# Moving one group's loads, transpositions and cluster steps half a unit and more later in a fused attention and FFN kernel

## Chip, cores, metric

The kernel runs on one core of a Trainium2 chip. The metric is the time of one execution on the device in microseconds (us). The kernel before has a median of 328.62 us over 13 runs (327.7 to 329.52).

## What is computed

Routing attention over 4 batches of 8 heads, 768 positions, head size 64, and then a gated FFN over the 3072 tokens (512 to 1536 to 512):

```python
q_assign = np.argmax(np.einsum('bhsd,hcd->bhsc', q_n, c_n), axis=-1)
k_assign = np.argmax(np.einsum('bhsd,hcd->bhsc', k_n, c_n), axis=-1)
mask = q_assign[:, :, :, None] == k_assign[:, :, None, :]
scores = scale * np.matmul(q, k.transpose(0, 1, 3, 2))
scores = np.where(mask, scores, -1000000000.0)
attn = softmax(scores)
x = np.matmul(attn, v)            # heads side by side: (3072, 512)
xn = x / rms(x) * rms_g
g = xn @ w_gate
out = (g * sigmoid(g) * (xn @ w_val)) @ w_out
```

A query sees only keys of its own cluster, one of 16 for each head. The kernel gets the mask by appending a one-hot row of the cluster to q and to k, so that one matmul of 64 + 16 rows gives score and mask together.

## The kernel before, in words

All counting is from 0. There are 32 heads, n = 0 to 31, in 8 **groups** g of four, so that batch b has groups 2b and 2b+1. There are 8 **units** u: unit u is half of the queries (384) of batch u // 2, with all eight heads. Unit u therefore needs the groups of batch u // 2, both of them. The "fifth group" is g = 4, heads 16 to 19, first needed by unit 4. The "second unit" is u = 1.

The program writes out the order of every engine by hand. One call of `attention` (L659) runs through the 24 **gaps** of a unit: at each gap TensorE gets a pair of score matmuls (L348, three pairs a head), ScalarE the exp of them (L352), and in between comes the probability times v of the head before (`pv`, L366, 18 matmuls). Two heads share one accumulator `acc` in PSUM, of which there is one. VectorE empties it when both heads are in: reciprocal `inv` (L371) and product `x` (L373). The `pv` of the next pair cannot start before that.

Between the score pairs a list called `fill` is laid out. Each entry is a weight and a function, and entries are taken as long as their summed weight keeps step with the gaps. In unit u it holds, in this order:

1. the last eight gate/val items of the FFN of unit u-2 (f = 8 to 11): `gv`, L444, followed on VectorE by L453 (`th`) and L457 (`gvT`), with ScalarE's tanh (L452) between
2. `rms(u-1)`: ScalarE's squares (L393), VectorE's small steps (L400, L144 to L153) and the three products `xn` (L403), and then on SP's queue the x transposition, a DMA from `xn` to `xnT` (L406)
3. loads of heads listed in `LATE`
4. the output projection of unit u-2, nine items (`out_mm`, L469), whose result ScalarE copies (L472) and SP stores (L473)
5. the first sixteen gate/val items of unit u-1.

The preparation of group g = u + 2 is spread among these. It has **rows** and **clusters**. The sixteen rows are, for each head, two transpositions on VectorE (`trans`, L217, for heads from 14 on; they wait for the head's loads), then casts on POOL into the bf16 operands `qext` and `kext` (L240) and of v (L243), and with them SP's loads of v for head n + 4 and of q and k for head n + 6 (`load_v`, L107; `load_qk`, L96, eight DMAs a head of 48 KB each). Six staging buffers hold q and k. The clusters are, for q and for k: the products with the centroids on TensorE (`sc`, L254), a transposition (L257), the maximum (L262), a comparison (L266), a scaling for k (L285) and a transposition back (`oh`, L286) on VectorE, and sixteen small DMAs on POOL's queue that put the one-hot rows into `qext` and `kext` (`place`, L297).

The gate, val, o, and sc results share three PSUM buffers (`gen`), which are used in turn. Group 3 is prepared in unit 1, with its last steps at the head of unit 2. The three parts of `wo`, the last weight, are loaded on POOL's queue (L207) in unit 1 too.

The lines that the change touches decide where the parts of a group's preparation go:

```python
LATE = [19] + [n for n in range(20, B * H) if n % HG < 2]        # L58
if u == 2:                                                       # L703
    fill = fill[:1] + spread(fill[1:], [(0.0, f) for _, f in a3[5:]])
n = 12 if u == 2 else len(rows)                                  # L708
fill += spread(o, rows[:n]) + spread(ffn[:CUT], [(0.0, f) for _, f in rows[n:]] + clusters)
```

`spread(a, b)` lays the entries of b evenly among those of a. So in unit 2 twelve of the rows stand in the output projection and four with the clusters in the FFN part, and in later units all sixteen stand in the output projection.

Of the kernel before, what the change touches and what calls it, by code (L numbers as in the profile page):

```python
# [22 lines left out]
def kernel(  # L23
# [13 lines left out]
    B, H, S, D = q.shape  # L37
# [7 lines left out]
    HG = 4  # L45
# [8 lines left out]
    CUT = 2 * FC - 8  # L54
    LEAD = 6
    NQ, NV = 6, 8
    AV = 4
    LATE = [19] + [n for n in range(20, B * H) if n % HG < 2]  # L58
    BH = 14
    BG = BH // HG  # L60

# [22 lines left out]
    def load(n, part, on=None):  # L84
        if n not in staged:
            staged[n] = stage.tile([P, 2, ST, D], F32, tag="qk", name="qk")
        if n < BH:
            (on or nc.sync).dma_start(out=staged[n][:, part], in_=src((q, k)[part], n))
            return

        to = staged[n][:, part].rearrange("p t d -> p (t d)").rearrange("p (i r d) -> p i r d", i=HT, d=32)
        of = (q, k)[part][n // H, n % H].rearrange("(r p i e) (c d) -> e c p i r d", p=32, i=HT, e=2, d=32)
        for e in range(2):
            for c in range(2):
                r = 32 * (2 * e + c)
                nc.sync.dma_start(out=to[r:r + 32], in_=of[e, c])  # L96

    def load_qk(n):
        if n < B * H:
            load(n, 0)  # L100
            load(n, 1)

    def load_v(n, vq=None):
        if n >= B * H:
            return
        stagedv[n] = stage.tile([P, ST, D], F32, tag="vs", name="vs", bufs=NV)
        (vq or nc.sync).dma_start(out=stagedv[n], in_=src(v, n))  # L107
# [98 lines left out]
    def load_o(c):  # L206
        nc.gpsimd.dma_start(out=wo[:, c:c + 4], in_=moe_w_out[c * P:(c + 4) * P].rearrange("(c p) f -> p c f", p=P))  # L207
# [4 lines left out]
    def trans(g, h, part, on=None):  # L212
        if (g, h // 2) not in qkT:
            qkT[g, h // 2] = qk32.tile([P, 2, 2, UQ], F32, tag="qkT", name="qkT")
        qk = staged[g * HG + h]
        if g * HG + h >= BH:
            nc.vector.transpose(qkT[g, h // 2][:, h % 2, part], qk[:, part].rearrange("p t d -> p (t d)"))  # L217
            return
        ps = ps_g.tile([P, UQ], F32, tag="gen", name="tq")
        for i in range(HT):  # L220
            nc.tensor.transpose(ps[:, i * P:(i + 1) * P], qk[:, part, 2 * i:2 * i + 2].rearrange("p t d -> p (t d)"),
                                ident_f)
        to, by = qkT[g, h // 2][:, h % 2, part], 1.0 / ZS if part and g < BG else 1.0
        if on is nc.vector:
            nc.vector.tensor_scalar_mul(to, ps, by)  # L225
        else:
            nc.scalar.activation(to, ps, ACT.Copy, scale=by)
# [5 lines left out]
    def cast(on, g, h, part, es=(0, 1)):  # L233
        for e in es:
            to = cols((kext if part else qext)[g % 4][:D, h], g, e)
            of = qkT[g, h // 2][e * D:(e + 1) * D, h % 2, part]
            if on is nc.scalar:
                nc.scalar.copy(to, of)
            else:
                on.tensor_copy(to, of)  # L240

    def vcast(n):
        nc.gpsimd.tensor_copy(vbf[n // HG % 4][:, n % HG, :, :D], stagedv[n])  # L243
# [24 lines left out]
    def cluster_steps(g, m):  # L268

        of = {}  # L270

        def products():
            of["cl"] = cluster_products(g, [(h, m) for h in range(HG)])

        def most():
            of["mx"] = largest(of["cl"])

        def same():
            of["ohT"] = asg.tile([P, UQ], BF16, tag="ohT", name="ohT", bufs=2)
            compare(of["ohT"].rearrange("p (b e c) -> p b e c", e=2, c=NC), of["cl"], of["mx"])  # L280

        def back():
            put[g, m] = asg.tile([P, UQ], BF16, tag="oh", name="oh", bufs=3)
            if m and g >= BG:
                nc.vector.tensor_scalar_mul(of["ohT"], of["ohT"], ZS)  # L285
            nc.vector.transpose(put[g, m], of["ohT"])  # L286

        return [products, most, same, back]
# [3 lines left out]
    def place(on, g, m, es=(0, 1)):  # L292

        ext = (kext if m else qext)[g % 4]
        for h in range(HG):
            for e in es:
                on.dma_start(out=ext[D:D + NC, h, e * UQ:(e + 1) * UQ],  # L297
                             in_=put[g, m][32 * h + e * NC:32 * h + (e + 1) * NC])
# [190 lines left out]
    def group_work(g):  # L489

        t, c = [], []
        for h in range(HG):
            n = g * HG + h
            w = 0.0 if n >= BH else 0.3
            t += [(w, lambda h=h: trans(g, h, 0)), (w, lambda h=h: trans(g, h, 1))]

            def others(n=n):
                vcast(n)
                load_v(n + AV)
                if n + NQ not in LATE:  # L500
                    load_qk(n + NQ)

            def both(h=h, f=others):
                cast(nc.gpsimd, g, h, 0)
                f()
                cast(nc.gpsimd if g * HG + h >= BH else nc.vector, g, h, 1, (0,))
            if g == 2:
                c.append((0.0, others))
            else:
                c += [(0.0, both), (0.0, lambda h=h: cast(nc.gpsimd if g * HG + h >= BH else nc.vector, g, h, 1, (1,)))]  # L510
        a = []
        for m in range(2):
            a += [(0.0 if i else 0.7, f) for i, f in enumerate(cluster_steps(g, m))]
            if g == 3:
                a.append((0.0, lambda m=m: place(nc.gpsimd, g, m)))
            elif g == 2:
                a.append((0.0, (lambda: (place(nc.gpsimd, g, 1), place(nc.gpsimd, g, 0, (1,)))) if m else
                          (lambda: place(nc.gpsimd, g, 0, (0,)))))
        if g > 3:
            a[:1] = [(1.4, lambda f=(a[0][1], a.pop(4)[1]): [x() for x in f])]  # L520
            a.append((0.0, lambda: [place(nc.gpsimd, g, m) for m in range(2)]))
        return t, c, a
# [12 lines left out]
    def spread(a, b):  # L535

        if not a:
            return list(b)
        w, n = [], 0
        for i, x in enumerate(a):  # L540
            w.append(x)
            while n < len(b) * (i + 1) // len(a):
                w.append(b[n])
                n += 1
        return w

    def ffn_work(u):
        n = UNITS[u][2] / HT
        return [(0.64 * n, lambda f=f, val=val: gv(u, f, val)) for f in range(FC) for val in (False, True)]

    def out_work(u):
        return [(0.86, lambda t=t, p=p: out_mm(u, t, p)) for t in range(UNITS[u][2]) for p in range(3)]
# [127 lines left out]
    for u in range(1, NU):  # L680
        ffn, o, g = ffn_work(u - 1), out_work(u - 2) if u > 1 else [], u + 2
        if u == 1:
            t, c, a = group_work(2)
            t3, c3, a3 = group_work(3)
            n = LEAD - 4
            o3 = [(0.0, lambda i=i: load_o(i)) for i in range(0, FC, 4)]
            prep = c + a + spread(weave(t3[n:], c3), o3) + a3[:5]
            idle = const.tile([P, 1], BF16)

            def norm():  # L690
                rms(0)
                nc.gpsimd.tensor_copy(idle, xn[0][:, CC - 1, HT - 1, P - 1:])
                for h in range(HG):
                    casts(pool_, H + h, K0, Q0, K1, Q1)

            hooks = {(1, 0, 0): late[6], (1, 0, 1): lambda: (late[7](), norm())}
            hooks.update({(1, *divmod(2 + i, HT)): t3[i][1] for i in range(n)})
            hooks[1, *divmod(LEAD - 1, HT)] = lambda: xtrans_all(0)
            fill = spread(ffn[:CUT], prep)
            attention([(1, h) for h in range(H)], fill, LEAD, hooks)  # L700
        else:
            fill = ffn_work(u - 2)[CUT:]
            if u == 2:  # L703
                fill = fill[:1] + spread(fill[1:], [(0.0, f) for _, f in a3[5:]])
            fill.append((0.0, lambda u=u: rms(u - 1)))
            rows, clusters = group(g)
            fill += [(0.0, lambda n=n: load_qk(n)) for n in LATE if n - n % HG == (u + 3) * HG or (u, n) == (2, 19)]
            n = 12 if u == 2 else len(rows)  # L708
            fill += spread(o, rows[:n]) + spread(ffn[:CUT], [(0.0, f) for _, f in rows[n:]] + clusters)
            attention([(u, h) for h in range(H)], fill, 1 if g < NG else 0, ahead=1)  # L710
    rest = ffn_work(NU - 2)[CUT:]
    rest[0][1]()
# [39 lines left out]
```

## Time and profile before

| what | value |
|---|---|
| median of 13 runs | 328.62 us |
| profiled execution, its own time | 329.52 us |
| profiled execution, span | 327.7 us |
| clock of TensorE | 1.00 |
| TensorE in the chain that ended last | 78% of the span |
| VectorE in that chain | 10% |
| DMA in that chain | 3%, nearly all of it wo |
| SP's queue: q and k loads of 48 KB, issue to landing | 2.8 and 2.7 us (median) |
| x transposition, issue to landing | 3.7 / 3.8 / 5.1 us (least, median, most) |
| place DMAs, issue to landing | 2.5 and 2.4 us |

The span is the time from the first to the last instruction in the profile of one execution; the time of the same execution is 1.8 us longer. Busy time counts what an engine executes and not its waits. Of a row in order of time, the first number is the start in us from the start of the span. Where instructions are merged, the length covers all of them. In this profile unit 2 begins at about 66 us and unit 3 at about 104, and each later unit up to unit 6 takes about 37 us as well.

### The profile page before, as it was taken

The page shows a single profiled execution, that of the slowest core. Times are in us where ns is not written, and L with a number is a line of the kernel's source. Part 1 is how long each engine was busy: PE and PEld are TensorE (multiplying, and loading weights), DVE is VectorE, ACT ScalarE, POOL GpSimd, SP SyncE. Part 2 cuts the span into 40 slices and gives each one's busy share as a digit, 9 for nine tenths or more (in the row PEclk, how much of TensorE's full clock was granted, in tenths as well). Part 3 has the DMA queues.
Part 4 walks back from the last instruction along what each step waited for, and adds up shares of the span by engine and source line. Part 5 has one row for each costly group of instructions (what it writes and reads, how often), then busy time and mean ns, then how long its engine had stood idle before and what let it go on. Part 6 is the DMA issues. An engine that isn't in the chain of part 4 may idle for free.

```text
span 327.7 us, 7794 instructions
## 1 busy us (share of the span) xinstructions
PE 319.0 (97%) x2851; PEld 191.7 (59%) x2865; DVE 222.5 (68%) x509; ACT 246.0 (75%) x425; POOL 137.5 (42%) x277
## 2 busy tenths in 40 slices
PE   7999899998999999999999999999999999999996
PEld 4546656654556555665566655665566656655654
DVE  5999978879378785877678694976265644685430
ACT  4899988977778867897778877798779868863322
POOL 5999499994935356450926347350000000000000
DMA  7999995799546554571545540000700040001002
GB/s 245 373 277 185 226 188 98 120 183 188 98 67 137 137 121 70 104 174 55 102 85 128 147 114 34 6 21 1 147 2 0 2 112 34 0 2 74 25 1 96
DMA packets 88742, 34.24 MB, mean 104 GB/s; under 512 B 70400, under 2 KB 85632, under 8 KB 88704
## 3 DMA queue, kind: packets, MB, share of 16 engines
q1 hardware_dynamic: 79536, 27.45, 35.4%
q0 software_dynamic: 8880, 5.91, 11.3%
q8 instruction: 22, 0.36, 0.5%
q10 hardware_dynamic: 288, 0.39, 0.4%
q14 instruction: 16, 0.13, 0.1%
HBM read 28.61 MB, written 6.29 MB: 106 GB/s over the span
## 4 chain that ended last, share of the span: by engine, by line
PE 78%; DVE 10%; POOL 4%; DMA 3%; issue 2%; ACT 2%; DVEq 0%; ACTq 0%
PE o L469 18%; PE gate L444 17%; PE val L444 16%; PE s L348 15%; PE acc L366 8%; DMA wo<-in_moe_w_out_dram 3%; PE sc L254 2%; POOL qext L240 1%; POOL kext L297 1%; DVE kext L332 1%; DVE qext L332 1%; DVE pads L327 1%; DMA boot<-in_centroids_dram 1%; DVE x L373 1%; PE o L480 1%
## 5 line engine op out<-in xcount | busy, mean ns | idle before, releaser
L352 ACT ACTIVATE pT<-s,off 128x768 bf16<-128x768 f32 x192 | 170.9, 904 | 31.0 <-PE s L348 30.3
L348 PE MATMUL s<-qext,kext 80*128 80x384 bf16 x384 | 94.9, 328 | 1.5 <-ACT pT L352 0.8
L444 PE MATMUL gate<-xnT,wg 128*128 128x384 bf16 x384 | 78.3, 326 | 0.1
L444 PE MATMUL val<-xnT,wv 128*128 128x384 bf16 x384 | 78.1, 326 | 0.0
L453 DVE SCALAR_TENSOR_TENSOR th<-th,gate 128x384 f32<-128x384 f32 x84 | 46.3, 551 | 34.8 <-ACT th L452 34.2
L469 PE MATMUL o<-wo,gvT 128*128 128x512 bf16 x262 | 66.3, 379 | 1.7 <-DMA wo<-in_moe_w_out_dram 1.0
L348 PEld LDWEIGHTS <-kext 80*128 80x128 bf16 x384 | 36.4, 98 | 35.1 <-issue 7.5
L452 ACT ACTIVATE th<-gate 128x384 f32<-128x384 f32 x84 | 41.2, 490 | 15.3 <-PE gate L444 14.5
L457 DVE SCALAR_TENSOR_TENSOR gvT<-th,val 128x384 bf16<-128x384 f32 x84 | 46.2, 551 | 9.3 <-PE val L444 3.4
L444 PEld LDWEIGHTS <-wg 128*128 128x128 bf16 x384 | 36.1, 97 | 23.4 <-issue 0.8
L366 PEld LDWEIGHTS <-pT 128*128 128x128 bf16 x1152 | 43.4, 97 | 10.1 <-DVE x L373 1.1
L444 PEld LDWEIGHTS <-wv 128*128 128x128 bf16 x384 | 35.6, 97 | 22.5 <-issue 0.6
L240 POOL CAST qext<-qkT 64x384 bf16<-64x384 f32 x64 | 35.3, 558 | 30.8 <-DVE inv L371 18.4
L366 PE MATMUL acc<-vbf,pT 128*128 128x65 bf16 x1152 | 45.7, 193 | 0.6 <-ACT pT L352 0.2
L469 PEld LDWEIGHTS <-gvT 128*128 128x128 bf16 x276 | 26.0, 97 | 26.6 <-issue 1.1
L297 POOL DMA_DIRECT2D qext<-oh x48 | 23.0, 488 | 33.7 <-DVE oh L286 29.1
L240 POOL CAST kext<-qkT 64x384 bf16<-64x384 f32 x58 | 31.4, 541 | 4.4 <-DVE qkT L225 2.5
L472 ACT COPY o_sb<-o 128x512 f32<-128x512 f32 x23 | 13.5, 585 | 17.0 <-PE o L469 17.0
L297 POOL DMA_DIRECT2D kext<-oh x48 | 23.1, 488 | 7.4 <-DVE oh L286 7.1
L371 DVE RECIPROCAL inv<-acc 128x6 f32<-128x6 f32 x32 | 6.0, 188 | 24.8 <-PE acc L366 24.4
L373 DVE TENSOR_TENSOR x<-acc,inv 128x384 f32<-128x384 f32 x32 | 17.8, 557 | 1.1
L217 DVE STREAM_TRANSPOSE qkT<-qk 128x384 f32<-128x384 f32 x36 | 18.1, 549 | 0.0
(83 smaller groups left out, 229.0 us busy)
## 6 DMA issues: line engine op xcount, KB each, us to landing
vs<-in_v_dram SPq DMA_DIRECT2D x32, 192.0 KB, 4.2
out_dram<-o_sb SPq DMA_DIRECT2D x23, 256.0 KB, 2.7
qk<-in_q_dram SPq DMA_DIRECT2D x72, 48.0 KB, 2.8
qk<-in_k_dram SPq DMA_DIRECT2D x72, 48.0 KB, 2.7
qk<-in_q_dram SPq DMA_DIRECT2D x14, 192.0 KB, 4.2
qk<-in_k_dram SPq DMA_DIRECT2D x12, 192.0 KB, 4.2
wg<-in_moe_w_gate_dram POOLq DMA_DIRECT2D x4, 384.0 KB, 9.0
wv<-in_moe_w_val_dram POOLq DMA_DIRECT2D x4, 384.0 KB, 10.4
```

The costliest lines, as they stand in the source:

```text
L217: nc.vector.transpose(qkT[g, h // 2][:, h % 2, part], qk[:, part].rearrange("p t d -> p (t d)"))
L240: on.tensor_copy(to, of)
L297: on.dma_start(out=ext[D:D + NC, h, e * UQ:(e + 1) * UQ], in_=put[g, m][32 * h + e * NC:32 * h + (e + 1) * NC])
L348: nc.tensor.matmul(ps[:, j, :w] if nt == HT else flat[:, j * w:(j + 1) * w], lhsT=cols(kext[g % 4][:KR, hh], g, kc // HT, kc % HT * P, (kc ...
L352: nc.scalar.activation(pT[u, h][:, n * i:n * i + n, :w], of, ACT.Exp, bias=off, scale=scale if g >= BG else scale * ZS)
L366: nc.tensor.matmul(acc[:, h % 2, t], lhsT=pT[u, h][:, kc, t * P:(t + 1) * P], rhs=vbf[g % 4][:, hh, kc % HT * 2 + kc // HT], start=kc == 0 ...
L373: nc.vector.tensor_tensor(dst, acc[:, :, :nt, :D], inv[:, :, :nt].unsqueeze(3).broadcast_to([P, 2, nt, D]), op=ALU.mult)
L444: nc.tensor.matmul(ps, lhsT=w[:, c, f * P:(f + 1) * P], rhs=xnT[u][:, c, :n], start=c == 0, stop=c == CC - 1)
L452: nc.scalar.activation(th, ps, ACT.Tanh, scale=0.5)
L453: nc.vector.scalar_tensor_tensor(th, th, 1.0, ps, op0=ALU.add, op1=ALU.mult)
L457: nc.vector.scalar_tensor_tensor(gvT[u][:, f, :n], gates[u], 0.5, ps, op0=ALU.mult, op1=ALU.mult)
L469: nc.tensor.matmul(outs[u], lhsT=gvT[u][:, f, t * P:(t + 1) * P], rhs=wo[:, f], start=f == 0, stop=f == FC - 1)
```

## The change

```diff
-    LATE = [19] + [n for n in range(20, B * H) if n % HG < 2]
+    LATE = {2: (17, 18, 19, 20, 21), 3: (23, 24, 25), 4: (28, 29)}
...
-                if n + NQ not in LATE:
+                if not any(n + NQ in x for x in LATE.values()):
                     load_qk(n + NQ)
...
             fill = ffn_work(u - 2)[CUT:]
-            if u == 2:
-                fill = fill[:1] + spread(fill[1:], [(0.0, f) for _, f in a3[5:]])
+            if u in (2, 3):
+                fill = fill[:1] + spread(fill[1:], [(0.0, f) for _, f in a3[5:]] if u == 2 else c4)
             fill.append((0.0, lambda u=u: rms(u - 1)))
             rows, clusters = group(g)
-            fill += [(0.0, lambda n=n: load_qk(n)) for n in LATE if n - n % HG == (u + 3) * HG or (u, n) == (2, 19)]
-            n = 12 if u == 2 else len(rows)
-            fill += spread(o, rows[:n]) + spread(ffn[:CUT], [(0.0, f) for _, f in rows[n:]] + clusters)
+            fill += [(0.0, lambda n=n: load_qk(n)) for n in LATE.get(u, ())]
+            rows = [(0.0, f) for _, f in rows]
+            if u == 2:
+                fill += o + spread(ffn[:CUT], rows)
+                c4 = clusters
+            else:
+                n = 12 if u == 3 else len(rows)
+                fill += spread(o, rows[:n]) + spread(ffn[:CUT], rows[n:] + clusters)
```

- Heads 17 and 18, loaded within unit 1 before, are loaded in unit 2 behind `rms(1)` and its x transposition, ahead of heads 19, 20 and 21, which stay there. Head 23, loaded within unit 2 before, is loaded in unit 3 behind that unit's x transposition, ahead of 24 and 25. Head 22 and all others keep their place in the program.
- All sixteen rows of group 4 stand in the FFN part of unit 2, one beside each gate/val item. The output projection of unit 2 has none.
- The clusters of group 4 (`c4`) stand at the head of unit 3, among the last seven gate/val items of unit 1's FFN and so ahead of `rms(2)`. They keep the weight 1.4 of their first entry, so the fill of unit 2 weighs 1.4 less and that of unit 3 1.4 more.
- Of group 5, twelve rows stand in the output projection of unit 3 and the four of head 23 with the clusters in its FFN part. From unit 4 on the order is as before.

The work itself, its sizes and its buffers stay as they are.

## The prediction

> **What bounds it now.** I read the busy shares first, then busy time stretch by stretch, the list of waits, and the order of time around what those point at.
>
> ```profile
> PE 319.0 (97%) x2851; PEld 191.7 (59%) x2865; DVE 222.5 (68%) x509; ACT 246.0 (75%) x425; POOL 137.5 (42%) x277
> ```
>
> TensorE is busy 319.0 of 327.7 us. By stretch (columns: length, then busy time and count of PE, PEld, DVE, ACT, POOL; clock; DMA share; GB/s):
>
> ```profile
> 76.00:113.00 37.00, 35.93 (x333) 21.63 (x334) 26.43 (x59) 28.16 (x47) 21.78 (x45) 1.00 0.61 118
> 113.00:150.20 37.20, 37.09 (x340) 22.26 (x341) 27.31 (x62) 29.41 (x53) 17.47 (x36) 1.00 0.56 123
> ```
>
> Each stretch is as long as a unit. The second has 0.11 us without a matmul, the first 1.07. So the span moves by what TensorE waits or stops waiting for, and here nearly all of that is one wait. From the rows in order of time of SP, POOL and TensorE (start, length, engine, line, operation, count, and in brackets the idle time before it and who ended it):
>
> ```profile
> 67.31 3.04 SPq L96 DMA_DIRECT2D qk<-in_q_dram  x4
> 69.66 0.74 POOL L207 DMA_DIRECT2D wo<-in_moe_w_out_dram  x1
> 70.40 4.44 SPq L96 DMA_DIRECT2D qk<-in_k_dram  x4
> 74.94 1.59 SPq L107 DMA_DIRECT2D vs<-in_v_dram  x3
> 78.14 1.02 PE L469 MATMUL o<-wo,gvT 128*128 128x512 bf16 x4 [0.97 <-DMA wo<-in_moe_w_out_dram]
> ```
>
> The last third of wo is issued at 69.66 and needed at 77.17, but is in only at 78.1. Beside it SP loads head 18 (the eight at 67.31 and 70.40) and three heads of v; head 17 went just before. The DMA share is 1.2 to 1.3 from 64 to 78 us.
>
> **Part 1: heads 17, 18 leave this stretch; gain 0.97.** Sixteen SP DMAs go from before 75 us to behind the x transposition at 79.52, past four v loads. Before 79.52 SP then holds only those v loads, which issue by about 65. The three wo loads take 6.1, 7.9 and 8.4 us to land; the 6.1 is the first one, with less beside it. At 6.1 the last lands at 75.8, 1.2 ahead of need. Ends: 0 gained (8.4 again) or 0.97; I take 0.97, as half the traffic beside it is gone. No other wait of TensorE of any size lies in that stretch: 1.07 idle less 0.97 is 0.10.
>
> **Part 2: nothing of group 4 in unit 2's output projection.** Six stream transpositions (L217, 0.55 each) leave VectorE's queue there, and POOL's casts of the same heads move along. VectorE sits idle 4.6 us behind them before, so no time comes of it. One thing there needs watching: the order on TensorE shifts, since the fill of unit 2 is 1.4 lighter in its own weights. The first pv group of a new pair (L366), which needs the accumulator that L373 empties, comes at 80.57 (running the new order from 74.08 with a score pair 0.33, a pv 0.545, four gate, val or o matmuls 0.65, 0.65, 0.86) instead of 82.57. L373, without the L217 ahead of it, ends at about 80.0. It holds by 0.5: cost 0.
>
> **Part 3: group 4 in the FFN part of unit 2.** Eight L217 among 16 gate/val items replace 5 us of cluster work there, so VectorE has less to do. They now wait on loads: SP takes 5.3 to 6.3 us a head (81.25 to 98.60 for three, before). Head 17's k lands near 90 and is wanted at 93; 18's at 95, wanted 97; 19's (last issue 98.0, plus 2.75 to landing) at 100.7, wanted at 100.5. A VectorE wait of 0.2 there is covered: the next tile that TensorE needs back is the gate of th 1.5 us later. Cost 0; without cover up to 0.3.
>
> **Part 4: group 4's cluster steps at the head of unit 3; loss 0.76.** TensorE's sixteen records of sc (1.43 us) move from unit 2 to unit 3, sum 0. VectorE gets two scT, two mx, two ohT, one scaling and two oh (5 us) between the last four gate/val pairs of unit 1's FFN, just ahead of the RMS norm. That chain before:
>
> ```profile
> 112.11 0.55 DVE L453 SCALAR_TENSOR_TENSOR th<-th,gate 128x384 f32<-128x384 f32 x1 [0.62 <-ACT th L452]
> 112.77 0.56 DVE L457 SCALAR_TENSOR_TENSOR gvT<-th,val 128x384 bf16<-128x384 f32 x1
> 113.77 0.17 DVE L400 SCALAR_TENSOR_TENSOR ms<-ss 128x3 f32<-128x3 f32 x1 [0.44 <-ACT xn L393]
> ...
> 117.54 0.57 DVE L217 STREAM_TRANSPOSE qkT<-qk 128x384 f32<-128x384 f32 x1
> 118.03 0.16 DVE L371 RECIPROCAL inv<-acc 128x6 f32<-128x6 f32 x1
> 118.22 0.56 DVE L373 TENSOR_TENSOR x<-acc,inv 128x384 f32<-128x384 f32 x1
> ```
>
> and what stands against it: the next pair's pv on TensorE
>
> ```profile
> 119.74 0.71 PE L366 MATMUL acc<-vbf,pT 128*128 128x65 bf16 x18
> ```
>
> Slack 0.96: x ends at 118.78. Now the new order, counted from G, the start of the gate of f=10. VectorE: th at G+1.45 (1.57 and 1.37 for the last two gates before). From there it never idles: th 0.47, oh(q) 0.50, gvT 0.47, mx 0.46, th 0.47, ohT 0.55, gvT 0.47, scaling 0.29, oh(k) 0.50 (start to start, where two follow each other in the trace) makes ms at G+5.63. The norm takes 3.77 (113.77 to 117.54), inv 0.19, x 0.56: x ends at G+10.15. TensorE: gate, s, val, gate, s, val 3.26, o 0.86, s 0.33, pv 0.545, o, s, o, s 2.38, two o parts 1.73, s 0.33: it wants the accumulator at G+9.44, because in the new order a pv stands one o part earlier. It waits 0.71 and a release of 0.05. A wait of this kind and its release (22.78 to 22.83) are seen near the start of the kernel:
>
> ```profile
> 22.22 0.56 DVE L373 TENSOR_TENSOR x<-acc,inv 128x384 f32<-128x384 f32 x1
> 22.83 0.60 PEld L366 LDWEIGHTS <-pT 128*128 128x128 bf16 x18 [0.50 <-DVE x L373]
> ```
>
> Behind the waiting pv stand o parts and all later scores. Nine spacings and one lag of 0.1 either way: 0.4 to 1.1. The three gen buffers of PSUM hold: the tightest, o after gvT of f=10, has 0.2. ScalarE's squares end before ms.
>
> A rule weighs here. The Trainium skill (Perfetto Trace Analysis, Identifying the Most-Contended Engine) says matmul busy time overstates how close TensorE is to its limit and LDWEIGHTS busy should be read; at 59% it would leave room in which 0.76 vanishes, and the sum would be -0.97. The row says 37.09 of 37.20 with matmuls back to back: no room, -0.21. I take the row.
>
> **Part 5: SP's queue in unit 2 and POOL.** Between the two x transpositions SP had five heads, three outs, four v, without a gap from 81.25 to 114.59, then idled until 117.77, when xn was ready. Now six heads (17 to 22). The same skill page (What "DMA-bound" means) warns that a solid issuing track is itself the bound: then one more head is 5.3 more, 119.9. By rows at their shortest (0.655 a load, 0.66 an out, 0.47 a v: 31.4+2.0+1.9) SP is free at 116.5; at the pace before, near 119. xn is ready at about 118. I take 119: landing 3.8 later is 122.8, the first gate of unit 2's FFN wants it at 123.3 plus the 0.76. Even the rule's 119.9 lands at 123.7, ahead of 124.1. Cost 0; without cover, up to 1.5. Head 23's k, behind it, lands near 128 and is wanted by VectorE near 127.7, where 1.5 us of slack covers it. The outs of unit 2 go from 98.7 to about 110, and ScalarE rewrites that buffer from 115.5: covered. POOL: sixteen place DMAs at 0.48 run from 110.6 to 118.4, then group 5's casts start, 118.25 before. Unit 4 reads group 4 after 140: covered.
>
> **Sum.** -0.97 + 0.76 = -0.21 us against the profiled execution: span 327.7 to 327.5, its own time 329.52 to 329.3. The median of the runs is 0.9 below that execution, so 328.62 - 0.21 = 328.4.
>
> **Rivals.** (a) *The pv doesn't wait*, or below 0.3: if VectorE's chain is shorter, or ScalarE delivers th sooner. For it: the slack before was 0.96. Against: the count leaves no idle in which 0.5 could be found. 327.65 to 327.95. (b) *SP is late*, the slower end: it decides from the moment the transposition of unit 2 is issued after 120.2. If every head takes the 6.0 of the slower ones, 36 + 3.9 + 81.25 is 121.2, landing at 125.0 to 126.0 (3.8 to 4.8): 0.9 to 1.9 of TensorE on top, and head 23 then holds VectorE too. For it: no gap in SP's row. Against: group 4's place DMAs no longer compete there. 329.3 to 330.3. (c) *wo is late all the same*: the v loads, now earlier, and the place DMAs hold it. Then only the loss stays, 329.4. Against: a head's 3072 packets of 128 bytes are gone. (d) Head 19 or 23 reaches VectorE over 1.5 us late: 0.3 to 1 on top, 328.7 to 329.4.
>
> **Numbers.** Forecast, with its own range 328.0 to 328.9: 0.43. (a) 0.24, (b) 0.21, (c) 0.05, (d) 0.07. A measurement can tell about 0.2% (0.66 us) from no change. Faster (below 327.96): (a) and a little of the forecast, 0.27. Slower (above 329.28): (b), (c), half of (d) and tails, 0.31. Same: 0.42. Range 327.5 to 330.0 takes in (a) and most of (b).
>
> **What would show it.** The wait of o L469 for wo gone, the last wo landing in under 7.3 us; a wait of pv L366 for x L373 of 0.4 to 1.1 us once, near 118; no second of that kind; SP's transposition of unit 2 issued between 118 and 120; PE of every other unit within 0.2 of its length. Wrong if the pv wait is missing, if the gate after the transposition waits, or if TensorE waits for a gen buffer between 104 and 112.

## The result, and the profile after

The changed kernel takes 330.97 us (median of 11 runs, 329.65 to 331.71) against 328.67 for the kernel before (48 runs, 327.47 to 330.08). The ratio is 1.0066, 95% interval 1.0054 to 1.0079: slower by 1.8 to 2.6 us, where 328.4 was forecast. The profiled execution took 330.65 with a span of 328.6; before it was 329.52 and 327.7.

The same two views as before, busy shares and busy time by stretch, of the changed kernel:

```profile
PE 319.0 (97%) x2851; PEld 191.4 (58%) x2865; DVE 221.5 (67%) x509; ACT 246.2 (75%) x425; POOL 137.5 (42%) x277
```

```profile
76.00:113.00 37.00, 36.56 (x343) 21.97 (x344) 25.53 (x60) 29.50 (x52) 15.58 (x33) 1.00 0.46 84
113.00:150.20 37.20, 35.51 (x328) 21.21 (x326) 26.39 (x63) 27.09 (x44) 23.18 (x48) 1.00 0.68 131
```

TensorE's work is the same 319.0 us. Its idle time in the first stretch fell from 1.07 to 0.44; in the second it grew from 0.11 to 1.69. The list of waits of the changed kernel (total, times, longest; `acc` L366 is the pv, which waits for `x`) names two that the kernel before hardly had, and wo is no longer in it:

```profile
PE gate L444 <- DMA xnT<-xn: 1.3, 1, 1.3
PE acc L366 <- DVE x L373: 0.9, 3, 0.4
```

TensorE in order of time, changed kernel:

```profile
76.52 1.02 PE L469 MATMUL o<-wo,gvT 128*128 128x512 bf16 x4
...
80.58 0.72 PE L366 MATMUL acc<-vbf,pT 128*128 128x65 bf16 x18 [0.33 <-DVE x L373]
...
118.30 0.71 PE L366 MATMUL acc<-vbf,pT 128*128 128x65 bf16 x18 [0.38 <-DVE x L373]
...
125.25 0.81 PE L444 MATMUL gate<-xnT,wg 128*128 128x384 bf16 x4 [1.26 <-DMA xnT<-xn]
```

The first o part runs without its wait. One pv waits in unit 2 and one in unit 3 (the third of the list, 0.15, is near the start), and then the first gate of unit 2's FFN waits for the x transposition. The bracket counts from the modelled end of the matmul before, some 0.16 after the next could have started, so the cost on the path (the start compared with the same place in a kernel without the wait, see the table below) is about 0.5, 0.54 and 1.42. VectorE's last step of xn, and SP's queue ahead of that gate, changed kernel:

```profile
115.47 2.08 DVE L403 SCALAR_TENSOR_TENSOR xn<-x,n,grow 128x512 bf16<-128x512 f32 x3
...
112.25 2.71 SPq L96 DMA_DIRECT2D qk<-in_q_dram  x4
115.00 2.62 SPq L96 DMA_DIRECT2D qk<-in_k_dram  x4
117.73 1.52 SPq L107 DMA_DIRECT2D vs<-in_v_dram  x3
119.41 2.25 SPq L406 DMA_TRANSPOSE xnT<-xn  x1
```

and the changed kernel's transfer of the tile xnT from 112 to 135 us (one transfer, so the three numbers agree):

```profile
DMA to landing us min/median/max: 5.8/5.8/5.8
```

The same of the kernel before:

```profile
113.73 0.86 SPq L107 DMA_DIRECT2D vs<-in_v_dram  x2
117.77 1.49 SPq L406 DMA_TRANSPOSE xnT<-xn  x1
...
DMA to landing us min/median/max: 3.8/3.8/3.8
```

VectorE had finished xn at 117.55, but SP issued head 22 and three loads of v first. The transposition went out 1.86 late, and it landed 5.8 us after its issue, at 125.21. The same transfer took 3.8 in the kernel before. There the last v loads had gone out at 113.73, 4 us ahead of the transposition, and here three stand directly in front of it.

**A measure by parts.** Behind the first gate of unit 3's FFN every run here is alike: the span less that gate's start is 166.1 to 166.2 us. The time to the first gate of unit 0's FFN goes from 40.6 to 43.6 from one execution to the next, whatever the kernel. In between lies what the change touches. X, Y and Z are the stretches between the first gates of the FFN of units 0, 1, 2 and 3, as the start times in the traces give them:

| kernel | X | Y | Z | sum | ratio to before, 95% |
|---|---|---|---|---|---|
| before | 45.69 | 37.17 | 37.16 | 120.02 | |
| before again (e11, e13, e14) | 45.03, 45.69, 45.07 | 37.17 | 37.16 | 119.36, 120.02, 119.40 | |
| changed | 45.06 | 39.12 | 37.16 | 121.34 | 1.0066 [1.0054, 1.0079] |
| changed again (e1) | 45.06 | 39.06 | 37.16 | 121.28 | 1.0038 [1.0023, 1.0053] |
| changed, third (e15) | 45.06 | 39.41 | 37.72 | 122.19 | |
| e2 v first | 45.06 | 38.16 | 37.70 | 120.92 | 1.0064 [1.0044, 1.0084] |
| e3 v behind | 45.05 | 37.70 | 38.57 | 121.32 | 1.0068 [1.0053, 1.0082] |
| e4 weights | 44.95 | 37.99 | 37.66 | 120.60 | 1.0040 [1.0022, 1.0057] |
| e5 without Part 1 | 45.30 | 37.71 | 37.17 | 120.18 | 1.0019 [1.0007, 1.0031] |
| e6 head 22 late | 45.05 | 38.01 | 39.21 | 122.27 | 1.0087 [1.0066, 1.0107] |
| e7 the same, weights | 44.56 | 37.17 | 39.11 | 120.84 | 1.0067 [1.0041, 1.0094] |
| e8 before, v behind | 46.31 | 37.16 | 37.17 | 120.64 | 0.9994 [0.9979, 1.0009] |
| e9 head 18 only, weights | 44.56 | 37.16 | 37.16 | 118.88 | 1.0006 [0.9993, 1.0020] |
| e9 again (e16) | 45.13 | 37.17 | 37.16 | 119.46 | |
| e10 without Part 1, weights | 45.29 | 37.16 | 37.16 | 119.61 | 1.0002 [0.9990, 1.0015] |
| e12 before, head 18 late | 44.56 | 40.90 | 37.16 | 122.62 | 1.0087 [1.0072, 1.0102] |

The least of each, 44.56, 37.16 and 37.16, is what TensorE takes with no wait. Most of what stands above it is one of the waits named here.

Two cautions. The ratios come from several series of runs: the changed kernel has 1.0066 in one and 1.0038 in another, and their intervals do not meet. Taken together they put the loss between 0.8 and 2.6 us, and ratios of different series that differ by 0.3% tell nothing; the stretches do. And a profile is one execution: that of e8 was the longest of its 15 runs, those of e7 and e9 the shortest of their 6 and 22.

### The profile page after: what moved, and what is told of

It reads as the page before. It is cut to its first block, busy times and chain, and to the rows that moved or that the text cites. A ratio compares the mean times of both kernels' runs of the same rounds, so it can differ in the third digit from the quotient of the medians.

```text
span 328.6 us, 7790 instructions
## 1 busy us (share of the span) xinstructions
PE 319.0 (97%) x2851; PEld 191.4 (58%) x2865; DVE 221.5 (67%) x509; ACT 246.2 (75%) x425; POOL 137.5 (42%) x277
## 4 chain that ended last, share of the span: by engine, by line
PE 79%; DVE 12%; ACT 3%; DMA 3%; issue 2%; DVEq 0%; ACTq 0%
PE gate L444 18%; PE val L444 18%; PE s L348 15%; PE o L469 14%; PE acc L366 9%; PE sc L254 3%; DVE xn L403 2%; DMA xnT<-xn 2%; ACT pT L352 1%; DVE kext L332 1%; DVE qext L332 1%; DVE x L373 1%; DVE pads L327 1%; DMA boot<-in_centroids_dram 1%; PE o L480 1%
## 5 line engine op out<-in xcount | busy, mean ns | idle before, releaser
L366 PEld LDWEIGHTS <-pT 128*128 128x128 bf16 x1152 | 43.3, 97 | 11.2 <-DVE x L373 1.8
L366 PE MATMUL acc<-vbf,pT 128*128 128x65 bf16 x1152 | 45.7, 193 | 1.3 <-DVE x L373 0.9
L217 DVE STREAM_TRANSPOSE qkT<-qk 128x384 f32<-128x384 f32 x36 | 18.6, 554 | 0.7 <-DMA qk<-in_k_dram 0.7
L373 DVE TENSOR_TENSOR x<-acc,inv 128x384 f32<-128x384 f32 x32 | 17.8, 558 | 1.1
```

Source lines behind the costliest of these rows:

```text
L366: nc.tensor.matmul(acc[:, h % 2, t], lhsT=pT[u, h][:, kc, t * P:(t + 1) * P], rhs=vbf[g % 4][:, hh, kc % HT * 2 + kc // HT], start=kc == 0 ...
L373: nc.vector.tensor_tensor(dst, acc[:, :, :nt, :D], inv[:, :, :nt].unsqueeze(3).broadcast_to([P, 2, nt, D]), op=ALU.mult)
```

## The experiments

Two theories stood against each other at first. **A**: the loss is SP's queue, which is one head longer between the two x transpositions; the transposition of unit 2 goes out late. **B**: it is the cluster steps at the head of unit 3, through VectorE. Unless said otherwise the edit is to the changed kernel, all of the computation is done, and the ratio is in the table.

**e1, e15: the changed kernel again**, unaltered.

> The changed kernel unaltered, for its own variation and for a second profile. Theory A (SP's queue makes the x transposition of unit 2 late, and the first gate of unit 2's FFN waits for it): that wait again, 1.0 to 2.5 us, transposition issued at 119 to 120 and landing in over 5 us; time 1.005 to 1.008 of before. Rival B (the waits of pv for x, 0.3 and 0.5 us in the first profile, carry the loss, and the gate's wait is chance): gate wait under 0.5 in this profile and the time still above before.

> The changed kernel, unaltered, a third profile. If its loss belongs to the kernel, the gate near 125 again waits 1.0 to 1.4 for the transposition (issued at 119.2 to 119.8, landing 5.5 to 6.2), the pv waits are there, wo doesn't wait, and the segment takes 121.1 to 121.5; if the first two profiles were chance, the gate waits under 0.8 and the segment takes under 120.8.

e1 is the first profile over again: issued at 119.56, landing 6.0, gate wait 1.19, sum 121.28. In e15 the order of time on SP and TensorE shows another way to the same end:

```profile
118.69 2.91 SPq L107 DMA_DIRECT2D vs<-in_v_dram  x3
121.77 1.88 SPq L406 DMA_TRANSPOSE xnT<-xn  x1
...
126.04 0.81 PE L444 MATMUL gate<-xnT,wg 128*128 128x384 bf16 x4 [1.55 <-DMA xnT<-xn]
```

The v loads took 2.91 us to issue and not 1.52. The transposition left at 121.77 and landed in 4.2, so xnT was there at 126.0. Late by its issue alone, or by issue and landing, the gate waits 1.2 to 1.55 in all three profiles. The loss belongs to the kernel, though the expected issue and landing were missed in e15, and its sum of 122.19 lies above the expected 121.1 to 121.5.

**e2, e3: where the v loads of heads 20 to 23 stand.** They are taken out of the rows and put right behind unit 1's x transposition (e2), or right behind unit 2's (e3).

```diff
-                load_v(n + AV)
+                if n // HG != 4:
+                    load_v(n + AV)
...
+            if u == 2:          # e3: u == 3
+                fill += [(0.0, lambda n=n: load_v(n)) for n in range(20, 24)]
```

> The changed kernel with the four loads of v for heads 20 to 23 issued right behind the x transposition of unit 1, ahead of heads 17 to 21, instead of behind head 22. SP has as much to issue as before, but no large loads directly ahead of the transposition of unit 2. If the lateness of issue is what costs (A1): transposition issued at 119 to 119.5 as before, landing still over 5 us, gate wait 1.2 to 1.5, time as the changed kernel's. If its slow landing beside the v loads costs (A2): landing in 3.8 to 4.2, at 123.3, gate wait under 0.2, time 1.3 to 1.6 us below the changed kernel, about 329.4. B: same as the changed kernel.

> The changed kernel with the same four loads of v moved behind the x transposition of unit 2 (into unit 3). SP's queue is shorter by 1.9 us. A1 and A2: transposition issued at 117.6, landing 3.8 later at 121.4, gate wait gone, time 1.4 us below the changed kernel in the profile, 329.3 to 329.6; left of the loss are the two pv waits of 0.3 and 0.5 against the gain of 0.97, so no more than before. B: time as the changed kernel's, 331.

SP in e2 and then in e3:

```profile
119.20 2.65 SPq L96 DMA_DIRECT2D qk<-in_k_dram  x4
122.01 2.46 SPq L406 DMA_TRANSPOSE xnT<-xn  x1
```

```profile
118.39 1.45 SPq L406 DMA_TRANSPOSE xnT<-xn  x1
119.94 3.31 SPq L107 DMA_DIRECT2D vs<-in_v_dram  x4
```

In e2 it is no earlier (unit 0's first gate is 2.2 later in this execution, so 122.01 is about 119.8 on the clock of the changed kernel), but it lands in 4.2. In e3 SP is ready in time and it lands in 5.7, with the v loads behind it. Neither gate waits for it. In e3 the slack covers the landing, and in e2 TensorE comes later too, behind a val that waited 0.30 for VectorE near 106 (0.46 on the path); without that the gate would have waited about 0.2. So with an issue near 119.4 it takes both, the late issue and the long landing, to make the 1.4; e15 makes it with a later issue alone. Neither kernel is faster, because waits come back at other steps: in e2 the one near 106 and 0.29 at 132.69, in e3 one of 1.14. TensorE in e3:

```profile
131.59 0.81 PE L444 MATMUL gate<-xnT,wg 128*128 128x384 bf16 x4 [1.14 <-DVE gvT L457]
```

VectorE stands there in an L217 that waits 1.57 for head 23's k, which SP loads behind the transposition.

**e5: Part 1 alone undone.**

```diff
-    LATE = {2: (17, 18, 19, 20, 21), 3: (23, 24, 25), 4: (28, 29)}
+    LATE = {2: (19, 20, 21), 3: (23, 24, 25), 4: (28, 29)}
```

> The changed kernel, but heads 17 and 18 are loaded in the second unit as before, so SP has five heads between the two x transpositions and not six. (A) SP's queue one head longer is the largest part of the loss: the x transposition of unit 2 is issued at about 117.7 when xn is ready and lands 3.8 to 4.3 later, the gate at about 124 waits less than 0.3 for it, the wo wait comes back at 0.8 to 1.0, the pv waits of 0.3 to 0.5 in units 2 and 3 stay. From the first gate of unit 0 to the first gate of unit 3, which takes 120.02 before and 121.3 in the changed kernel, 120.4 to 120.9; time 1.001 to 1.003 of before. (B) The clusters at the head of unit 3 are what is slow, by whatever way: 121.0 to 121.5, ratio 1.004 to 1.007. (C) The landing is long because of the v loads beside it and not because of the queue: issued at 117.7, landing still 5.5 to 6, gate wait 0.5 to 1 less what the slack covers, 120.9 to 121.4.

The heads are miscounted in this text: between the transpositions the changed kernel has six, the kernel before five, and e5 four. SP is done early and the transposition leaves when xn is ready. TensorE and SP in e5:

```profile
77.62 0.59 PE L469 MATMUL o<-wo,gvT 128*128 128x512 bf16 x2 [0.59 <-DMA wo<-in_moe_w_out_dram]
118.30 1.49 SPq L406 DMA_TRANSPOSE xnT<-xn  x1
118.91 0.71 PE L366 MATMUL acc<-vbf,pT 128*128 128x65 bf16 x18 [0.38 <-DVE x L373]
```

Y falls from 39.12 to 37.71, and what is left above 37.16 is the pv wait. The cluster steps are still at the head of unit 3, so B explains 0.54 of the loss in Y and no more. A explains the rest: 1.4. The landing stayed at 5.6 without any v load near it, which A did not expect.

**e4, e10: the order of the score pairs.** The weight of 1.4 that the clusters had in unit 2 stays there, on the rows, and they weigh nothing in unit 3. TensorE's score pairs then stand against the o parts as they did before the change. e10 has e5's edit on top.

```diff
-            rows = [(0.0, f) for _, f in rows]
+            rows = [(1.4 / 16 if u == 2 else 0.0, f) for _, f in rows]
...
-                c4 = clusters
+                c4 = [(0.0, f) for _, f in clusters]
```

> The changed kernel with the weight of 1.4 left in unit 2 (1.4/16 on each row) and taken off the cluster steps in unit 3, so that TensorE's order around the projections is that of before and the pv comes one o part later. Both theories: no wait of pv for x at 80 and at 118. A: the gate still waits for the transposition, now longer by what pv no longer waits, 1.8 to 2.2; time as the changed kernel's within 0.3 us. B: time 0.9 us below the changed kernel's.

> As e5 (17 and 18 loaded in the second unit, four heads on SP between the transpositions), with the weights of e4, so that the score pairs stand against the projections as before. (A) The pv wait of e5 near 118.9 is gone with the order and the wo wait is 0.5 to 1: segment 119.3 to 120.1, ratio 0.998 to 1.0005. (B) The pv wait belongs to the clusters on VectorE and stays near 0.5: segment 120.1 to 120.4, ratio 1.001 to 1.003.

Both pv waits are gone in both, while VectorE has the same cluster steps in the same order ahead of its norm. In e4 x (L373) starts at 117.23, 31.48 after unit 1's first gate, and in the changed kernel 31.56 after it, so VectorE delivers no sooner. The pv stands at 118.25, 32.50 after that gate, where the changed kernel's without its wait would stand at 31.63. So the wait comes from where the score pairs put the pv, and two lines of weights decide that. In e4 the gate still waits for the transposition, 0.66 and not the expected 1.8 to 2.2, as SP issued it 1.21 sooner counted from unit 1's first gate. And wo costs 0.39 in X although heads 17 and 18 are gone from that stretch:

```profile
123.74 0.81 PE L444 MATMUL gate<-xnT,wg 128*128 128x384 bf16 x4 [0.66 <-DMA xnT<-xn]
```

In e10 nothing is left but 0.57 for wo, and its ratio is 1.0002: no change. So with the score pairs in their old order and heads 17 and 18 where they were, the rest of the change costs nothing that shows here.

**e6, e7: head 22 late too**, with and without the weights.

```diff
-    LATE = {2: (17, 18, 19, 20, 21), 3: (23, 24, 25), 4: (28, 29)}
+    LATE = {2: (17, 18, 19, 20, 21), 3: (22, 23, 24, 25), 4: (28, 29)}
...
-                n = 12 if u == 3 else len(rows)
+                n = 8 if u == 3 else len(rows)
```

> The changed kernel, with head 22 also loaded behind the x transposition of unit 2, so SP has five heads between the transpositions again and three behind, and eight of the rows stand in unit 3's output projection. (A) Transposition issued at 117.7, landing 3.8 to 4.3, no gate wait for it; the pv waits of about 0.4 and 0.5 stay and the wo wait is gone; heads 22 and 23 reach VectorE up to 1.5 later, which a gate near 130 pays with up to 0.6. Segment 119.9 to 120.7, ratio 0.9995 to 1.002. (B) The lateness only moves: VectorE, held by the loads of 22 and 23, makes a gate near 130 wait 1 or more; segment 121 or more, ratio 1.003 and above. (C) The landing is 5.5 to 6 although the queue is short: gate wait about 0.7, segment 120.6 to 121.2.

> As the run before it, and unit 2 keeps the weight 1.4 of the clusters that moved (on its rows), and the clusters weigh nothing in unit 3, so the score pairs stand against the projections as they did in the kernel before. (A) No pv waits, no wait for the transposition, wo gone; what is left is up to 0.6 for head 23. Segment 119.1 to 119.9, ratio 0.997 to 0.9995: faster than before. (B) The lateness moves to heads 22 and 23: a gate near 130 waits 1 or more, segment 120 to 120.8, ratio 1.000 to 1.002. (C) The transposition comes late for another reason than the queue (landing 5.5 to 6): gate wait 0.5 to 0.9, segment 120.2 to 120.6.

B of both came true: with five heads between the transpositions the one of unit 2 leaves at once (117.87 and 116.20), but Z grows by 2. In e7 no gate waits for it. In e6 it lands after 6.4 us, at 124.27, and the gate starts at 124.30, 0.85 after the start of the pv ahead of it, where 0.54 is usual; so C's long landing came too, at half of C's cost. VectorE and TensorE in e6:

```profile
133.32 0.58 DVE L217 STREAM_TRANSPOSE qkT<-qk 128x384 f32<-128x384 f32 x1 [1.94 <-DMA qk<-in_k_dram]
...
134.39 1.51 PE L254 MATMUL sc<-qkT,cblk 128*32 128x384 f32 x16 [1.89 <-DVE th L453]
```

Four heads behind unit 2's transposition come too late for where their rows stand. VectorE's th comes next after the L217 of head 23 and starts at 133.82, when that is through. In e7 X and Y are at their least, and the whole 1.95 of its profile is lost here.

**e12: the kernel before, with only head 18's loads late.** Six heads on SP, and no other part of the change.

```diff
-    LATE = [19] + [n for n in range(20, B * H) if n % HG < 2]
+    LATE = [18, 19] + [n for n in range(20, B * H) if n % HG < 2]
```

> The kernel before, with only head 18's loads moved behind unit 1's x transposition: six heads on SP between the two transpositions as in the changed kernel, and no other part of the change. (A) SP's queue alone makes the loss: transposition of unit 2 issued at 119.2 to 120.2, landing 5 to 6, gate wait 0.8 to 1.8 for it; wo wait down to 0 to 0.7; no pv waits. Segment 120.3 to 121.3, ratio 1.001 to 1.005. (B) The queue costs nothing without the cluster steps: no gate wait over 0.3, segment 119.0 to 119.8, ratio 0.997 to 0.9995.

Neither theory's number holds, the sum is 2.6 to 3.3 above before, for a reason that comes sooner. VectorE and TensorE in e12:

```profile
85.64 0.58 DVE L217 STREAM_TRANSPOSE qkT<-qk 128x384 f32<-128x384 f32 x1 [4.18 <-DMA qk<-in_q_dram]
88.24 0.58 DVE L217 STREAM_TRANSPOSE qkT<-qk 128x384 f32<-128x384 f32 x1 [2.02 <-DMA qk<-in_k_dram]
...
90.01 1.44 PE L444 MATMUL val<-xnT,wv 128*128 128x384 bf16 x4 [1.91 <-DVE th L453]
```

Head 18's transpositions still stand in the output projection, before its loads can be there. This is what Parts 2 and 3 of the change are for: loads can go later only if the rows go with them. X is 44.56, so leaving out this one head removes the wo wait as the whole change does. The transposition of unit 2 left at 119.91 and took 6.2, but TensorE, 3.7 late, did not wait for it; so e12 can't test A.

**e8: the kernel before, with the v loads of heads 17 to 19 behind unit 1's x transposition.**

```diff
-                load_v(n + AV)
+                if n + AV not in (17, 18, 19):
+                    load_v(n + AV)
...
+            if u == 2:
+                fill += [(0.0, lambda n=n: load_v(n)) for n in (17, 18, 19)]
```

> The kernel before, with only the v loads of heads 17 to 19 moved, to behind the x transposition of unit 1 and the q and k of head 19. (A) The wo wait came of wo sharing the DMA engines with those loads: wo lands in 7.2 or less and the wait of 0.97 shrinks to 0 to 0.5; nothing else waits; segment 119.0 to 119.6, ratio 0.997 to 0.999. (B) wo is late because of the q and k loads of 17 and 18 alone: the wait stays at 0.8 to 1.0, segment 119.8 to 120.2, ratio 0.9995 to 1.0005. (C) The v loads then make the x transposition of unit 1 or head 20 late, and a gate near 87 or 95 waits: segment 120.3 or more.

wo waited 1.59 in this profile, the longest of 15 executions, and its thirds landed in 6.5, 7.7 and 9.1, with these v loads gone: they are not needed to make wo late. The median did not move within its interval, so that they add a little is not ruled out.

**e11, e13, e14: the kernel before again**, unaltered.

> The kernel before, unaltered: shows how far its segment repeats. Expected 119.8 to 120.2 (120.02 in the first profile), with the wo wait between 0.5 and 1.6 and no other over 0.35 between unit 0's and unit 3's first gate; the time to unit 0's first gate anywhere from 40.6 to 43.6, as in the others.

> The kernel before, unaltered, a third profile. If the wait of 0.97 for wo in the first profile belongs to that execution (its time of 329.52 is 0.9 above the median of 328.6), wo waits 0.5 or less here, the segment from unit 0's to unit 3's first gate takes 119.1 to 119.6 and the time is 328.0 to 329.0. If it belongs to the kernel, wo waits 0.8 to 1.1 and the segment takes 119.9 to 120.2.

> The kernel before, unaltered, a fourth profile: the same as for the third.

TensorE in e13, and then in e14:

```profile
79.96 1.02 PE L469 MATMUL o<-wo,gvT 128*128 128x512 bf16 x4 [0.97 <-DMA wo<-in_moe_w_out_dram]
```

```profile
79.51 1.02 PE L469 MATMUL o<-wo,gvT 128*128 128x512 bf16 x4 [0.36 <-DMA wo<-in_moe_w_out_dram]
```

The wait for wo has two sizes, 0.97 twice and 0.31 and 0.36; on the path 1.13 and about 0.5. Its mean there is 0.81, not 1.13. e11 missed its expected sum of 119.8 to 120.2 by this, with 119.36. The mean sum of the four is 119.70, that of the changed kernel's three 121.60: 1.9 longer, within the 1.8 to 2.6 of the medians. e13 and e14 took 331.38 and 330.9, since unit 0's first gate came at 43.4 and 43.5.

**e9, e16: head 18 alone late, with the weights.** Five heads between the transpositions, the rows moved as in the change.

```diff
-    LATE = {2: (17, 18, 19, 20, 21), 3: (23, 24, 25), 4: (28, 29)}
+    LATE = {2: (18, 19, 20, 21), 3: (23, 24, 25), 4: (28, 29)}
```

> The changed kernel, but of heads 17 and 18 only 18 is loaded late, so five heads stand on SP between the two x transpositions as in the kernel before (six in the changed kernel, four in e5, whose expectation counted five and six where it is four and six); and unit 2 keeps the weight 1.4 on its rows and the clusters weigh nothing in unit 3. (A) Queue length decides: transposition of unit 2 issued at about 117.5 when xn is ready, landing 3.8 to 4.5, no gate wait for it; no pv wait over 0.2; wo wait 0.2 to 0.7; head 23 not late by more than 0.3. Segment from unit 0's to unit 3's first gate 119.1 to 119.8 (before 120.02), ratio 0.997 to 0.9995. (B) Head 23, behind the transposition, is late all the same and a gate near 130 waits 0.4 to 1: segment 119.9 to 120.5, ratio 1.000 to 1.003. (C) wo comes 0.8 or more late again: 120 and more.

> The kernel of e9, a second profile; its first profile was the lowest of its 22 times (328.04, median 328.79). If that execution was a lucky one, a wait for wo of 0.2 to 0.8, or for head 23 of 0.2 to 0.8, or a later gate of unit 0 shows here and the segment takes 119.2 to 120; if not, the segment takes 118.8 to 119.0 and what differs is the time to unit 0's first gate, 41.5 and more.

The transposition leaves when xn is ready, at 116.73, lands in 4.4, and e9's first profile has no wait at all of those above: X, Y and Z at their least. Its second waits 0.41 for wo. So it is 0.5 shorter than the kernel before by the mean of the sums, and yet its median of 22 runs is not: 328.79 against 328.64. Two profiles don't tell which part of the other executions is longer, and that stays open. It is no faster than the kernel before, within 0.07% less and 0.2% more.

## Why the prediction was wrong

**Part 1 held** in the main: the wait went, though not by the margin it gave. In the changed kernel wo's thirds, in order, land in 7.1, 5.9 and 6.0, and nothing waits for the last one:

```profile
DMA to landing us min/median/max: 5.9/6.0/7.1
```

In e1 and e15 the last third took 7.4 and 7.6, over the 7.3 that the prediction named as its sign, and came up to 0.26 late; the pv wait at 80 hid that. The first third took 7.1 to 9.2 in the three profiles, against 6.1 to 6.8 in the four of before. Five v loads now issue just ahead of it (57.79 to 60.24), which fits rival (c), but no run here moved them alone. The size of the gain came from one execution that lay 0.9 above the median and had the larger of two waits. On the path it is 1.13 there, but 0.5 in others, so against the median the gain was overstated. With Part 2's wait, X is 45.06 in all three profiles of the changed kernel: 0.63 less than in two of before, and no less than in the other two.

**Part 5 is the step that failed**, with its "cost 0" for the transposition. "I take 119: landing 3.8 later is 122.8" had the issue nearly right: 119.41 and 119.56. It had the landing wrong, 5.8 and 6.0, and in the third profile the issue, 121.77. The gate could have started at 123.83, and xnT was there at 125.2 to 126.0: a cost of 1.42. A late issue with 3.8 would have been ready at 123.2, and a landing of 5.8 from the moment xn was ready, 117.55, at 123.35. Either alone was free; the sum was made with one of them at its value from a quieter queue. The row for 3.8 showed a transposition in front of which SP had stood idle, and that is not the state that one more head leads to.

What makes the landing long is not shown. Of the six profiles with v loads within 2 us of the transposition, five (changed, e1, e3, e4, e12) have 5.7 to 6.2, and e15, whose v loads took 2.91 to issue, 4.2. The others have 3.7 to 4.4, except e5 (5.6) and e6 (6.4), where SP had stood idle too; the same two with the old score order, e10 and e7, have 4.2 and 4.1. Group 4's place DMAs are no answer either. In rival (b) the prediction counted them as gone, but in the changed kernel they issue from 111.03 to 118.88, right ahead of the transposition. In e12 they were over by 111.73 and it took 6.2; in e5 and e10 they end alike, 1.0 and 0.9 behind its issue, and it took 5.6 and 4.2.

Rival (b) named the place and, with 0.9 to 1.9, the cost. Its deciding point, issue after 120.2, rested on the same 3.8; with 5.8 the point is 118.0. The rule weighed there, that a solid issuing track is itself the bound, gave 119.9 for the issue, about as near to 119.41 and 119.56 as the 119 taken, and said nothing of the landing.

**Part 4 held**: 0.76 predicted, 0.54 measured in each profile with the changed order, and e4 and e10 show that it hangs on the order of the score pairs. The room that the prediction read into the rule of LDWEIGHTS busy time, in which the wait would vanish, wasn't there: LDWEIGHTS was busy 58% in the changed kernel, and the waits still came through in Y. The rule is about the distance to the chip's peak rate; that a wait would vanish was the prediction's reading of it.

**Part 2 missed a wait of 0.5.** "L373 ... ends at about 80.0. It holds by 0.5": it ended at 80.53. VectorE and ScalarE in the changed kernel:

```profile
75.98 0.16 DVE L400 SCALAR_TENSOR_TENSOR ms<-ss 128x3 f32<-128x3 f32 x1 [0.87 <-ACT xn L393]
...
79.97 0.56 DVE L373 TENSOR_TENSOR x<-acc,inv 128x384 f32<-128x384 f32 x1
...
73.19 1.88 ACT L352 ACTIVATE pT<-s,off 128x768 bf16<-128x768 f32 x2
74.97 0.30 ACT L393 ACTIVATE xn<-x 128x128 bf16<-128x128 f32 x1
```

and in the kernel before:

```profile
75.52 0.15 DVE L400 SCALAR_TENSOR_TENSOR ms<-ss 128x3 f32<-128x3 f32 x1
...
73.69 0.89 ACT L352 ACTIVATE pT<-s,off 128x768 bf16<-128x768 f32 x1
74.47 0.31 ACT L393 ACTIVATE xn<-x 128x128 bf16<-128x128 f32 x1
```

The norm starts 0.46 later than before (75.52), though TensorE is 0.5 ahead. It waits for ScalarE's squares, which start at 74.97 behind two exps (74.47 before, behind one), since the same shift of the score pairs brought an exp forward. I followed TensorE and VectorE through the new order, and not ScalarE.

**Part 3** held: no wait in the changed kernel comes of group 4's L217. Head 23's k was predicted to land near 128 and wanted near 127.7; its L217 waited 0.65 for it and ran at 129.45. It cost nothing there, behind a gate that had already waited. In e3 and e4, with that wait gone or shorter, a gate further on pays 1.14 and 0.35, and in e15 0.30 although its gate had waited.

**Sum.** Against the profile of before: -1.13 (wo), +0.5 and +0.54 (pv), +1.42 (gate) is +1.33, and the table has 121.34 less 120.02, +1.32. Against the mean or the lesser executions of before, where wo costs 0.3 to 0.6 less, it is 1.6 to 2.0. The medians give 2.30 in one series and 1.36 in the other, so the waits account for the loss as well as it is known. Part 5 is 1.42 of it.

## What to carry to other kernels

When a queue gets longer ahead of a transfer that the bounding engine waits for, price its issue and its landing together, in the state that the longer queue leads to: here the landing time taken from a row with an idle queue in front of it was a lower end. If only the weights of a fill list change, follow the new order on all engines, since a score pair moved by one place also moves its exp in front of what the next engine wants. And take the size of a wait from several profiles before it is put down as a gain: here it was 0.97 in two of four and about a third of that in the others.

## What was not expected of the hardware

A wait of 1.91 us on TensorE in e12 was followed by half the clock. Busy time by stretch, e12 (the clock is the third number from the end):

```profile
88.00:90.00 2.00, 0.10 (x1) 0.00 (x0) 1.68 (x4) 0.77 (x2) 1.00 (x2) 1.00 0.45 71
90.00:92.00 2.00, 1.99 (x7) 0.98 (x7) 1.55 (x3) 0.00 (x0) 0.28 (x1) 0.50 0.49 77
92.00:93.00 1.00, 1.00 (x5) 0.48 (x4) 0.02 (x1) 0.82 (x1) 0.89 (x3) 0.50 0.41 63
93.00:94.00 1.00, 1.00 (x17) 0.62 (x15) 0.43 (x1) 0.68 (x3) 0.34 (x1) 0.79 0.46 72
```

From 90.01 to about 93.4 matmuls took about twice as long, which cost another 1.7 us: Y is 40.90 less 37.16, 3.74, and 2.07 of it is the wait on the path. The Trainium skill (TensorE: Matmul & The Clock Gate, Part 1) gives an idle window of about 3.4 us for this. Here half the clock followed a shorter wait; after 1.89 us in e6, and 1.59 in e8, the clock stayed at 1.00. What decides it is not shown. Of e12's five executions four have a mean clock of 0.994 or 0.995 and one 1.000, and that one is no shorter than the others (331.6 us, of 331.43 to 332.06).

The time to unit 0's first gate varies by 3 us between executions, and what sets it stays open. It is as large as anything measured here, so the waits and the stretches between fixed points told the kernels apart where single times could not.
